# Seven block products in place of eight for the 512-row expert blocks of a Fourier-mixing and mixture-of-experts kernel

## The chip, the core and the metric

The kernel runs on one NeuronCore of one Trainium2 chip. The metric is the device time of one execution in microseconds (us). A NeuronCore has a matmul engine (PE, TensorE), three engines for elementwise work (DVE or VectorE, ACT or ScalarE, POOL or GpSimd), an engine that here only issues transfers (SP), and 16 DMA engines. Each engine takes its instructions in the order in which the program emits them, and waits on semaphores for the others. [...]

## What is computed

The input x has 8 batches of 2496 rows of 256 values. Each batch goes through a Fourier transform over its rows and then over its columns, of which the real part is kept. Each of the 19968 resulting rows then goes to one of 8 experts, two matrix products with a relu between them, and is multiplied by its gate probability:

```python
X = np.fft.fft(np.fft.fft(x, axis=1), axis=2).real     # 8 x 2496 x 256
x = X.reshape(19968, 256)
logits = x @ w_gate
expert_idx = np.argmax(logits, axis=1)
gate_w = softmax(logits)[rows, expert_idx]
for e in range(8):                                     # x_sorted: rows by expert
    h = np.maximum(x_sorted[lo:hi] @ w1[e], 0.0)       # 256 -> 1024
    y_sorted[lo:hi] = h @ w2[e]                        # 1024 -> 256
return gate_w[:, None] * y                             # rows in their first order
```

All of it is in fp32.

## The kernel before

**Front end.** `first(b)` loads a batch, folds its mirrored rows and columns on DVE (`fold` and `fold_d`, L242 to L258) and does the first stage of the row transform; its result goes out to DRAM (`Td`) and comes back regrouped. `second(b)` does the second stage and the column transform: matmuls into PSUM tiles of the pool `pm_` (three buffers), copies to `z` on ACT, and, per step, two slices of 128 finished rows, one copied on ACT (L339) and one on DVE (L340). `route` (L346) finds expert and gate of each of the 10 x 128 rows of half a batch by small DVE operations, ranks the rows by matmuls (`rk`), and scatters each slice of 128 rows into the DRAM table `Xs` by an indirect DMA that POOL issues (`put_row`, L176). A row of `Xs` has W = 258 values: 256 of the row, its number in the output, and its gate.

**Experts.** `Xs` holds the rows by expert. `plan` writes tables that say at which row of `Xs` each block starts and which expert it has. `rounds` fixes the order and the sizes of the blocks: 2 of 256 rows and 4 of 128 after the first batch, 4 of 256 after the second, then 3, 5, 5, 5, 5 and 5 of 512 after the others, and 21 of 256 at the end; 59 in all, 28 of them of 512. The blocks of one round run while the front end of the batch after next is worked in between.

For each block `fetch` (L438) has SP load its rows (`xb`) and both weight matrices of its expert (`w1_sb`, `w2_sb`, 1 MB each, two buffers each), one block ahead. `turn` (L451) transposes the rows on TensorE into a PSUM tile and copies it to `xT` on DVE (L460). In `experts` (L463) layer 1 of a 512-row block is eight chunks of two products: the stationary operand is 128 x 128 of w1, the moving one 128 x 512 of `xT`, and the results `ph` leave PSUM through a relu to `hT`, by turns on DVE (L499) and ACT (L501). Layer 2 is four tiles of 128 rows, each eight products: stationary 128 x 128 of `hT`, moving 128 x 256 of w2. Its result `py` leaves through ACT (L513), which multiplies each row by its gate, and POOL scatters the tile to the output rows (`put_row` again). The next block's transposes stand between the tiles of layer 2. Two PSUM buffers each serve `ph` and `py`.

**Order.** The order on every engine is the order of emission, written by hand with generators. `experts` yields after each chunk of layer 1 (weight 1) and each tile of layer 2 (weight 2), 16 for a 512-row block. The main loop (L600 to L614) spreads the steps of the front end (`mixed`) over the expert work of a round: TICKS = 44 steps over the first 70% of the round's weight. Every fp32 matmul of the program stands in the profile as two MATMUL instructions on line L162, each with a weight load (PEld).

Of the kernel before, what the change touches and what calls it, by code (L numbers as in the profile page):

```python
# [11 lines left out]
F32 = mybir.dt.float32  # L12
BF16 = mybir.dt.bfloat16
I32 = mybir.dt.int32
ALU = mybir.AluOpType
ACTF = mybir.ActivationFunctionType
# [3 lines left out]
B, S, D = 8, 2496, 256  # L20
# [8 lines left out]
BIG, BLK = 512, 256  # L29
CAP = NT + BLK  # L30
ROWS = E * CAP + BLK
W = D + 2
NSL = 2 * HG
NY = D + 1
OUT = 1.0e6
# [6 lines left out]
def bc(ap, axis, n):  # L42
    shape = list(ap.shape)
    shape.insert(axis, n)
    return ap[tuple([slice(None)] * axis + [None])].to_broadcast(shape)
# [89 lines left out]
    return plan  # L135


TICKS = 44
MOST = max(k for now in rounds() for _, k, _ in now)


# [15 lines left out]
def kernel(ctx: ExitStack, tc, x, w_gate, w1, w2, out):  # L157
    nc = tc.nc
    vec, act, pool = nc.vector, nc.scalar, nc.gpsimd

    def mm(o, lhsT, rhs, start=True, stop=True):
        nc.tensor.matmul(o, lhsT=lhsT, rhs=rhs, start=start, stop=stop)  # L162

    Td = [nc.dram_tensor(f"Td{b}", (NR, 16 * D), F32, kind="Internal").ap() for b in range(B)]
    Xs = nc.dram_tensor("Xs", (ROWS, W), F32, kind="Internal").ap()
# [30 lines left out]
    bp = ctx.enter_context(tc.tile_pool(name="bp", bufs=2))  # L196
    pm_ = ctx.enter_context(tc.tile_pool(name="pm_", bufs=3, space=PSUM))
    pst = ctx.enter_context(tc.tile_pool(name="pst", bufs=1, space=PSUM))
    psh = ctx.enter_context(tc.tile_pool(name="psh", bufs=2, space=PSUM))
    psy = ctx.enter_context(tc.tile_pool(name="psy", bufs=2, space=PSUM))  # L200

    ix = cp.tile([NA, B * 4], I32, name="ix")
    at = (np.arange(B)[:, None] * (S // 4) + 7 - np.arange(4))[None]
# [142 lines left out]
    def route(b, h, rows, lg):  # L346

        nonlocal base

        def small(name, *dims, dt=F32):  # L350
            return sp.tile([128, *dims], dt, tag=name, name=name)

        mx, eq, v = small("mx", NSL), small("eq", NSL, E), small("v", NSL)
        vec.reduce_max(mx[:], lg[:], axis=AX_X)
        vec.tensor_tensor(eq[:], lg[:], bc(mx[:], 2, E), op=ALU.is_equal)
        vec.tensor_tensor(eq[:], eq[:], bc(con["rev"][:], 1, NSL), op=ALU.mult)
        vec.reduce_max(v[:], eq[:], axis=AX_X)
        vec.tensor_tensor(v[:], v[:], con["good"][:, h], op=ALU.mult)
        oh = small("oh", NSL + 1, E, dt=BF16)
        vec.memset(oh[:, NSL], 0.0)  # L360
        vec.tensor_tensor(oh[:, 0:NSL], bc(con["rev"][:], 1, NSL), bc(v[:], 2, E), op=ALU.is_equal)
        yield

        su = small("su", NSL)
        vec.tensor_tensor(lg[:], lg[:], bc(mx[:], 2, E), op=ALU.subtract)
        act.activation(lg[:], lg[:], ACTF.Exp)
        rk = pm_.tile([128, NSL + 1, E], F32, tag="m", name="rk")
        mm(rk[:], tri[:], oh[:], True, False)
        for s in range(NSL):
            mm(rk[:, s + 1:], ones[:], bc(oh[:, s], 1, NSL - s), False, s == NSL - 1)  # L370
        yield
        vec.reduce_sum(su[:], lg[:], axis=AX_X)
        vec.tensor_scalar(su[:], su[:], 1e-9, None, op0=ALU.add)
        vec.reciprocal(rows[:, :, D + 1], su[:])
        vec.tensor_scalar(rows[:, :, D], con["row"][:, h], float(b * S), None, op0=ALU.add)
        pos, pf, pi = small("pos", NSL, E), small("pf", NSL), small("pi", NSL, dt=I32)
        vec.tensor_tensor(pos[:], rk[:, 0:NSL], bc(base[:], 1, NSL), op=ALU.add)
        vec.tensor_tensor(pos[:], pos[:], oh[:, 0:NSL], op=ALU.mult)
        vec.reduce_sum(pf[:], pos[:], axis=AX_X)
        vec.tensor_tensor(pi[:], pf[:], con["far"][:, h], op=ALU.add)  # L380
        nxt = cp.tile([128, E], F32, tag="base", name="base", bufs=2)
        vec.tensor_tensor(nxt[:], rk[:, NSL], base[:], op=ALU.add)
        base = nxt
        for s in range(NSL):
            sent(put_row(Xs, pi[:, s:s + 1], rows[:, s], E * CAP - 1, "xs"), b)
            yield

# [50 lines left out]
    def fetch(b, size, tab, i):  # L438
        n = size // 128
        row = nc.sync.value_load(tab[:, 0, i:i + 1], min_val=0, max_val=ROWS - size)  # L440
        ev = nc.sync.value_load(tab[:, 1, i:i + 1], min_val=0, max_val=E - 1)
        xb = bp.tile([128, BIG // 128, W], F32, tag="xb", name="xb")
        taken(nc.sync.dma_start(out=xb[:, 0:n].rearrange("p t c -> p (t c)"),
                                in_=Xs[ds(row, size)].rearrange("(p t) c -> p (t c)", t=n)), b)
        w1_sb = bp.tile([128, 2, F], F32, tag="w1", name="w1_sb")
        nc.sync.dma_start(out=w1_sb[:], in_=w1[ds(ev, 1)].rearrange("o (c p) f -> p (o c) f", p=128))
        w2_sb = bp.tile([128, FC, D], F32, tag="w2", name="w2_sb")
        nc.sync.dma_start(out=w2_sb[:], in_=w2[ds(ev, 1)].rearrange("o (c p) d -> p (o c) d", p=128))
        return xb, w1_sb, w2_sb

    def turn(size, xb):  # L451

        xT = bp.tile([128, 2, BIG], F32, tag="xT", name="xT", bufs=1)
        n = min(size // 128, 2)
        for h in range(-(-size // 256)):
            pt = pst.tile([128, 2, n, 128], F32, tag="t", name="pt")
            for c in range(2):
                for t in range(n):
                    nc.tensor.transpose(pt[:, c, t], xb[:, 2 * h + t, c * 128:(c + 1) * 128], ident[:])  # L459
            vec.tensor_copy(xT[:, :, 256 * h:256 * h + 128 * n], pt[:].rearrange("p c t k -> p c (t k)"))  # L460
            yield xT

    def experts(todo):  # L463

        got, xT = None, None
        for k, (b, size, last, at) in enumerate(todo):
            n, m = size // 128, BIG // size
            if not k:  # L470
                while todo[0][:3] not in tabs:
                    yield 0
                got = fetch(b, size, tabs[b, size, last], at)
                for _ in range(9):
                    yield 0
                for xT in turn(size, got[0]):
                    pass
            xb, w1_sb, w2_sb = got
            got, turned = None, iter(())
            follow = todo[k + 1] if k + 1 < len(todo) else None  # L480

            def fetch_next():
                b, size, last, at = follow
                return fetch(b, size, tabs[b, size, last], at)

            if follow and follow[:3] in tabs:
                got = fetch_next()
            ro = bp.tile([128, BIG // 128], I32, tag="ro", name="ro", bufs=4)
            vec.tensor_copy(ro[:, 0:n], xb[:, 0:n, D])
            hT = bp.tile([128, FC, BIG], F32, tag="hT", name="hT", bufs=1)  # L490
            for f in range(FC // m):
                ph = psh.tile([128, m, size], F32, tag="h", name="ph")
                for j in range(m):
                    for c in range(2):
                        mm(ph[:, j], w1_sb[:, c, (m * f + j) * 128:(m * f + j + 1) * 128], xT[:, c, 0:size],
                           c == 0, c == 1)
                o = hT[:, m * f:m * (f + 1), 0:size]
                if f % 2:
                    vec.tensor_scalar(o, ph[:], 0.0, None, op0=ALU.max)  # L499
                else:  # L500
                    act.activation(o, ph[:], ACTF.Relu)  # L501
                yield 1
            if follow:
                while follow[:3] not in tabs:
                    yield 0
                got = got or fetch_next()
                turned = turn(follow[1], got[0])
            y = bp.tile([128, BIG // 128, D], F32, tag="y", name="y", bufs=3)
            for i in range(n):
                py = psy.tile([128, D], F32, tag="y", name="py")  # L510
                for f in range(FC):
                    mm(py[:], hT[:, f, i * 128:(i + 1) * 128], w2_sb[:, f], f == 0, f == FC - 1)
                act.activation(y[:, i], py[:], ACTF.Copy, scale=xb[:, i, D + 1:D + 2])  # L513
                put_row(out, ro[:, i:i + 1], y[:, i], NT - 1, "out")
                if i < n - 1 or n == 2:
                    xT = next(turned, xT)
                yield 2
            for xT in turned:
                pass

    def pads(b):
# [78 lines left out]
    for b in range(1, B):  # L600

        side, done, due = mixed(b), 0, 0.0
        if b == 1:
            side = woven(close(0), chain(early, side))
        total = 16 * sum(k * size for size, k, _ in rounds()[b - 1]) / BIG
        while done < total:
            w = next(work)
            done += w
            due += TICKS * w / (0.7 * total) if w else 1
            while due >= 1:  # L610
                next(side, None)
                due -= 1
        for _ in side:
            pass  # L614
# [27 lines left out]
```

## Time and profile before

| what | value |
|---|---|
| median of 10 runs | 1524.75 us (1519.35 to 1527.54) |
| the profiled execution | 1524.91 us |
| its span, first to last instruction | 1522.7 us |
| TensorE busy | 1435.8 us, 94% of the span |
| DVE, ACT, POOL busy | 390.8, 283.8, 379.9 us |
| layer 1 of all blocks (`ph`, L162) | 1888 instructions, 612.6 us |
| layer 2 of all blocks (`py`, L162) | 2720 instructions, 616.0 us |
| scatters to `Xs` and to the output (L177) | 160 and 170, 165.4 and 165.9 us |
| mean granted TensorE clock | 0.979 |
| DMA traffic | 234.19 MB, mean 154 GB/s |

The page of a profile gives for each engine its busy time, then the span in 40 slices with a digit for the busy tenths, then groups of equal instructions: line, engine, operation, output<-inputs, count, total busy time, mean duration in ns, and the idle time of the engine before them with what ended it. A timeline gives start, duration, engine, line and operation of each instruction or run of equal ones. Matmuls are pipelined, so the duration of one is longer than the distance between two starts. The time before the first 200 us and the very end aside, TensorE is nearly always busy; in the first 150 us it is busy for 99.8 us.

### The profile page before, as it was taken

How to read it: one execution, taken by the hardware profiler on the slowest of the kernel's cores; microseconds unless marked ns; L12 is line 12 of the kernel's file. 1: busy time of each engine (PE TensorE's matmuls, PEld its weight loads, DVE VectorE, ACT ScalarE, POOL GpSimd, SP SyncE). 2: the span in 40 equal slices, each digit the busy share in tenths (PEclk: the TensorE clock that was granted, in tenths of full speed). 3: DMA queues.
4: the chain of work that ended last, by engine and by line, in shares of the span. 5: the costliest groups of instructions: out<-in, count | busy, mean ns of one | idle time of the engine just before them, and what ended most of it. 6: DMA issues, size and time to landing. Idle time of an engine off the chain costs nothing.

```text
span 1522.7 us, 16870 instructions
## 1 busy us (share of the span) xinstructions
PE 1435.8 (94%) x6108; PEld 1068.9 (70%) x6108; DVE 390.8 (26%) x1139; ACT 283.8 (19%) x598; POOL 379.9 (25%) x382
## 2 busy tenths in 40 slices
PE   4759798998999999999999999999999999999998
PEld 2537687776676657776677677666766788888887
DVE  3462233342232223322232212123111111111111
ACT  1212122122122211221122112111111111111111
POOL 2344314322314311324122311331421111111111
PEclk9869999999999999999999999999999999999999
DMA  7648667736336442553434422532352255465451
GB/s 179 175 148 257 206 203 222 254 89 187 120 109 206 153 145 87 160 179 124 155 114 139 152 90 87 178 112 100 130 173 87 85 197 177 165 202 183 167 194 63
DMA packets 126131, 234.19 MB, mean 154 GB/s; under 512 B 12829, under 2 KB 85648, under 8 KB 126048
## 3 DMA queue, kind: packets, MB, share of 16 engines
q1 hardware_dynamic: 103491, 178.31, 36.4%
q0 software_dynamic: 20192, 53.43, 10.6%
q10 hardware_dynamic: 2365, 1.38, 0.4%
q8 instruction: 48, 0.79, 0.2%
q14 instruction: 35, 0.29, 0.1%
HBM read 179.15 MB, written 56.28 MB: 155 GB/s over the span
## 4 chain that ended last, share of the span: by engine, by line
PE 50%; issue 30%; POOL 6%; DVE 1%; POOLq 0%; ACT 0%
PE py L162 20%; PE ph L162 20%; PE p L162 5%; POOL out_dram L177 4%; PE s L162 2%; POOL Xs L177 1%; PE pt L459 1%; POOLq L177 0%; PE rk L162 0%; DVE xT L460 0%; ACT hT L501 0%; DVE hT L499 0%; PE pr L162 0%; POOLq L637 0%; DVE rows L340 0%
## 5 line engine op out<-in xcount | busy, mean ns | idle before, releaser
L162 PE MATMUL ph<-xT,w_sb 128*128 128x512 f32 (+2 forms) x1888 | 612.6, 478 | 15.8 <-issue 6.6
L162 PE MATMUL py<-w_sb,hT 128*128 128x256 f32 x2720 | 616.0, 381 | 8.2 <-DVE hT L499 6.6
L162 PEld LDWEIGHTS py<-w_sb,hT 128*128 128x128 f32 x2720 | 512.8, 191 | 84.7 <-issue 8.4
L162 PEld LDWEIGHTS ph<-xT,w_sb 128*128 128x128 f32 x1888 | 349.9, 192 | 230.1 <-issue 183.6
L177 POOL DMA_INDIRECT out_dram<-y,ro x170 | 165.9, 976 | 890.5 <-ACT y L513 822.0
L499 DVE TENSOR_SCALAR hT<-ph 128x512 f32<-128x512 f32 x170 | 117.6, 692 | 643.4 <-PE ph L162 355.5
L513 ACT ACTIVATE y<-py,xb 128x256 f32<-128x256 f32 x170 | 80.7, 475 | 620.7 <-PE py L162 592.9
L177 POOL DMA_INDIRECT Xs<-rows,pi x160 | 165.4, 1034 | 105.0 <-issue 55.0
L501 ACT ACTIVATE hT<-ph 128x512 f32<-128x512 f32 x170 | 101.6, 598 | 387.2 <-PE ph L162 362.1
L460 DVE COPY xT<-pt 128x512 f32<-128x512 f32 (+1 forms) x87 | 59.1, 680 | 252.5 <-PE pt L459 246.8
L162 PE MATMUL p<-rd,z 128*128 128x273 f32 x320 | 93.8, 419 | 8.5 <-ACT z L333 6.3
L162 PE MATMUL s<-xh,w 78*80 78x256 f32 (+2 forms) x262 | 76.8, 422 | 26.3 <-DVE xh L247 18.7
L340 DVE COPY rows<-p 128x256 f32<-128x256 f32 x80 | 34.0, 425 | 182.2 <-ACT rows L339 169.2
L162 PEld LDWEIGHTS s<-xh,w 78*80 78x80 f32 x262 | 43.2, 172 | 47.8 <-DVE xh L247 18.9
L162 PEld LDWEIGHTS p<-rd,z 128*128 128x128 f32 x320 | 59.0, 202 | 22.5 <-ACT z L333 8.4
L237 POOL DMA_INDIRECT xh<-in_x_dram,ix x31 | 31.9, 1028 | 136.7 <-PE s L162 121.6
L162 PEld LDWEIGHTS p<-m,t 128*128 128x128 f32 x320 | 49.0, 205 | 23.7 <-issue 13.2
L162 PE MATMUL p<-m,t 128*128 128x128 f32 x320 | 52.6, 294 | 5.7 <-ACT z L333 2.2
L459 PE MATMUL pt<-ident,xb 128*128 128x128 f32 x340 | 52.0, 275 | 2.7 <-DMA xb<-Xs 2.7
L459 PEld LDWEIGHTS pt<-ident,xb 128*128 128x128 f32 x340 | 43.1, 143 | 12.3 <-DMA xb<-Xs 3.5
L270 ACT COPY t<-s 80x512 f32<-80x512 f32 x64 | 37.0, 581 | 64.7 <-PE s L162 55.5
L339 ACT COPY rows<-p 128x256 f32<-128x256 f32 x80 | 29.9, 373 | 53.7 <-PE p L162 50.4
(89 smaller groups left out, 327.4 us busy)
## 6 DMA issues: line engine op xcount, KB each, us to landing
w_sb<-in_moe_w_dram SPq DMA_DIRECT2D x118, 1024.0 KB
xb<-Xs SPq DMA_DIRECT2D x28, 516.0 KB
Td<-t SPq DMA_DIRECT2D x32, 320.0 KB
t<-Td SPq DMA_DIRECT2D x16, 640.0 KB
xl<-in_x_dram SPq DMA_DIRECT2D x31, 312.0 KB
xb<-Xs SPq DMA_DIRECT2D x27, 258.0 KB
out_dram<-y,ro POOLq DMA_INDIRECT x170
Xs<-rows,pi POOLq DMA_INDIRECT x160
```

What stands on the lines that cost most here:

```text
L162: nc.tensor.matmul(o, lhsT=lhsT, rhs=rhs, start=start, stop=stop)
L177: return unordered(pool.indirect_dma_start(out=dst, out_offset=bass.IndirectOffsetOnAxis(ap=idx, axis=0), in_=rows, in_offset=None, bounds ...
L237: pool.indirect_dma_start(out=xh[:].rearrange("p j d -> p (j d)"), out_offset=None, in_=xrows, in_offset=bass.IndirectOffsetOnAxis(ap=ix[: ...
L270: act.copy(t1[:, 2 * half:2 * half + 2], ps[:])
L339: act.copy(rows[:, k, 0:D], p3[:, 0:D])
L340: vec.tensor_copy(rows[:, k + 1, 0:D], free(p3[:], D, [-1, D]))
L459: nc.tensor.transpose(pt[:, c, t], xb[:, 2 * h + t, c * 128:(c + 1) * 128], ident[:])
L460: vec.tensor_copy(xT[:, :, 256 * h:256 * h + 128 * n], pt[:].rearrange("p c t k -> p c (t k)"))
L499: vec.tensor_scalar(o, ph[:], 0.0, None, op0=ALU.max)
L501: act.activation(o, ph[:], ACTF.Relu)
L513: act.activation(y[:, i], py[:], ACTF.Copy, scale=xb[:, i, D + 1:D + 2])
```

## The change

The 512-row blocks take both layers in another way. A matrix product whose factors are each cut in 2 x 2 parts needs eight products of parts. With sums and differences of parts, seven products do (the form with 15 sums of Strassen and Winograd). For each layer the program forms four such sums of the left factor (`left`) and four of the right one (`right`), runs seven products, and adds them up to the four parts of the result (`seven`): three products accumulate in PSUM onto banks that already hold another one, and DVE adds the rest in five sums.

Layer 1's left factor is w1 (its sums are made on POOL, in `turn` for the next block), its right one is `xT`, cut in two times 256 rows (sums on DVE). Layer 2's left factor is the hidden layer (sums on DVE, with a relu in some of them), its right one w2, cut into 128 columns (sums on POOL, at the block's start). Layer 1 works in two halves (`g`) of two chunks; each half has a tile of 512 values in each of four PSUM banks, a, b, c and d, which replace the buffers of `ph` and `py`. The order of the hidden layer's last sums is set by `late`.

The gate is applied to the rows before they are scattered to `Xs` (ACT, in `route`), not to the results; the gate is positive, so it passes through the relu. `Xs` loses its column for the gate, W is 257. `route` yields five times more in each half batch. A 512-row block now yields a weight of 14, and TICKS is 52. The blocks of 256 and 128 rows keep their products, in the new PSUM banks, and their results leave by a plain copy. The transposed rows of 512-row blocks are copied to `xT` on ACT.

```diff
-W = D + 2
+W = D + 1
-TICKS = 44
+TICKS = 52
+HALVED = (512,)
...
-    psh = ctx.enter_context(tc.tile_pool(name="psh", bufs=2, space=PSUM))
-    psy = ctx.enter_context(tc.tile_pool(name="psy", bufs=2, space=PSUM))
+    pse = ctx.enter_context(tc.tile_pool(name="pse", bufs=1, space=PSUM))
...
-        vec.reciprocal(rows[:, :, D + 1], su[:])
+        vec.reciprocal(su[:], su[:])
+        yield
...
         for s in range(NSL):
+            act.activation(rows[:, s, 0:D], rows[:, s, 0:D], ACTF.Copy, scale=su[:, s:s + 1])
             sent(put_row(Xs, pi[:, s:s + 1], rows[:, s], E * CAP - 1, "xs"), b)
...
+    def left(eng, o, a11, a12, a21, a22):
+        eng.tensor_tensor(o[0], a21, a22, op=add)
+        eng.tensor_tensor(o[1], o[0], a11, op=sub)
+        eng.tensor_tensor(a21, a11, a21, op=sub)
+        eng.tensor_tensor(o[2], a12, o[1], op=sub)
+        return a11, a12, o[2], a22, o[0], o[1], a21
+
+    def right(eng, o, b11, b12, b21, b22, sign):
+        eng.tensor_tensor(o[0], b12, b11, op=sub)
+        eng.tensor_tensor(o[1], b22, o[0], op=sub)
+        third = (b22, b12) if sign > 0 else (b12, b22)
+        eng.tensor_tensor(b12, *third, op=sub)
+        eng.tensor_tensor(o[2], b21, o[1], op=sub)
+        return b11, b21, b22, o[2], o[0], o[1], b12
+
+    def seven(shape, product, out12, out21, out22, done, late=()):
+        n = int(np.prod(shape))
+        bank = {k: pse.tile([128, *shape], F32, tag=k, name=k) for k in "abcd"}
+        a, b, c, d = (bank[k] for k in "abcd")
...
+        product(0, a, True)
+        yield
+        product(5, b, True)
+        p1, u2, u4 = temp("p1"), temp("u2"), temp("u4")
+        act.copy(p1, a[:])
+        yield
+        product(4, c, True)
+        vec.tensor_tensor(u2, p1, b[:], op=add)
+        yield
+        product(6, d, True)
+        vec.tensor_tensor(u4, u2, c[:], op=add)
+        yield
+        product(1, a, False)
+        vec.tensor_tensor(out22, u4, d[:], op=add)
+        done(11, a)
+        done(22)
+        for f in late[:-1]:
+            f()
+        yield
+        product(2, c, False)
+        yield
+        product(3, d, False)
+        vec.tensor_tensor(out12, u2, c[:], op=add)
+        done(12)
+        for f in late[-1:]:
+            f()
+        vec.tensor_tensor(out21, u2, d[:], op=add)
+        done(21)
+        yield
...
     def turn(size, got):
...
+        if halved:
+            ws = bp.tile([128, 3, F // 2], F32, tag="ws", name="ws", bufs=1)
+            l = left(pool, [ws[:, k] for k in range(3)], *(w1_sb[:, c, k] for k in range(2) for c in range(2)))
+            yield
...
+            r = right(vec, [xs[:, k] for k in range(3)],
+                      *(xT[:, c, k * th:(k + 1) * th] for c in range(2) for k in range(2)), 1)
...
+    def two_layers(size, got, lr, xb, ro):
...
+        r2 = right(pool, [wt[:, k] for k in range(3)],
+                   *(w2_sb[:, c, :, k * H:(k + 1) * H] for c in range(2) for k in range(2)), -1)
...
+            def sums12(h11=h11, h12=h12, h22=h22, s1=s1, s2=s2):
+                vec.scalar_tensor_tensor(s1, h12, 0.0, h22, op0=ALU.max, op1=add)
+                vec.tensor_tensor(s2, s1, h11, op=sub)
+
+            def sums34(h11=h11, h12=h12, h21=h21, s2=s2, s4=s4):
+                vec.scalar_tensor_tensor(h12, h12, 0.0, h11, op0=ALU.max, op1=sub)
+                vec.tensor_tensor(s4, h21, s2, op=sub)
+
+            if (g + 1) * fp == FC // 2:
+                late = late + [sums12]
+                yield from seven((fp, th), product, h12, h21, h22, done, late)
+                sums34()
+            else:
+                yield from seven((fp, th), product, h12, h21, h22, done)
+                sums12()
+                late = [sums34]
+        l2 = [hid[:, 0], hid[:, 2], hs[:, 2], hid[:, 3], hs[:, 0], hs[:, 1], hid[:, 1]]
...
+        yield from seven((nt, H), product, y[:, 0:nt, H:], y[:, nt:2 * nt, 0:H], y[:, nt:2 * nt, H:], done)
...
-        total = 16 * sum(k * size for size, k, _ in rounds()[b - 1]) / BIG
+        total = sum(k * (14 if size in HALVED else 16) * size / BIG for size, k, _ in rounds()[b - 1])
```

Layer 2's products use the banks of layer 1's parts in the same order; `l2` says which part or sum of the hidden layer each of the seven products has as its stationary operand (h11, h21, s4, h22, s1, s2, h12).

## The prediction

> **What bounds the kernel now.** I read the page's head and its 40 slices first, to see whether one engine fills the time; then tables by stretch, to see where it does not; then the groups kept apart by shape, and last the timeline, for the true spacing of instructions.
>
> ```profile
> span 1522.7 us, 16870 instructions
> PE 1435.8 (94%) x6108; PEld 1068.9 (70%) x6108; DVE 390.8 (26%) x1139; ACT 283.8 (19%) x598; POOL 379.9 (25%) x382
> PE   4759798998999999999999999999999999999998
> ```
>
> ```profile
> 200.00:300.00 100.00, 92.79 (x465) 77.76 (x464) 37.38 (x121) 22.42 (x51) 33.31 (x33) 0.97 0.66 215
> 723.32:751.74 28.42, 28.42 (x105) 19.02 (x105) 4.22 (x7) 4.29 (x8) 3.90 (x4) 1.00 0.33 112
> 1200.00:1300.00 100.00, 100.00 (x473) 86.94 (x472) 14.36 (x27) 14.89 (x28) 14.34 (x15) 1.00 0.47 157
> ```
>
> Columns of the second fence: stretch and its length, then busy time and count of PE, PEld, DVE, ACT and POOL, the granted clock, DMA. The middle line is one 512-row block with no front-end work beside it: PE is busy for all of its 28.42 us and DVE for 4.22. TensorE's columns are the bound; every other engine has room, until it is given work that TensorE must wait for.
>
> ```profile
> 658.07 3.60 PE L162 MATMUL ph<-xT,w_sb 128*128 128x512 f32 x8
> 661.51 0.61 PE L162 MATMUL p<-m,t 128*128 128x128 f32 x4
> ...
> 182.19 3.84 PE L162 MATMUL ph<-xT,w_sb 128*128 128x128 f32 x32 [0.52 <-DVE ro L489]
> 185.86 3.62 PE L162 MATMUL py<-w_sb,hT 128*128 128x256 f32 x16
> 189.32 0.38 PE L459 MATMUL pt<-ident,xb 128*128 128x128 f32 x2
> ```
>
> Starts count here, since durations overlap. An fp32 product is two instructions. 512 columns: 3.44/8 = 0.430 us each. 256 columns: 3.46/16 = 0.2163. 128 columns, new weights each: 3.67/32 = 0.1147. A transpose: 0.44/4 = 0.11. A block before is 32 x 0.430 + 64 x 0.2163 + 8 x 0.11 = 13.76 + 13.84 + 0.88 = 28.48 us, and the stretch above says 28.42.
>
> **TensorE's part.** Layer 1 becomes 7 products x 4 chunks x 2 instructions = 56 of 256 columns: 12.11 us. Layer 2 becomes 7 x 8 x 2 = 112 of 128 columns: 12.85 us. With transposes 25.84, so 2.64 less a block; 28 such blocks save 73.9 us. Layer 2 gains only 1.0 us of its 13.84, because 128-column instructions come at the pace of their weights. The bounds for one are 0.110 (transposes) and 0.118 (a stretch of 32 loads in 3.76 us at 163.5): 28 x 112 x 0.008 = 25 us between them. I take 0.1147, the nearest shape.
>
> **DVE's part.** It gets 18 sums of 512 elements in layer 1, 5 of 256 in layer 2 and 4 of 256 on xT, and loses four evictions of 512 and two copies.
>
> ```profile
> L499 DVE TENSOR_SCALAR hT<-ph 128x512 f32<-128x512 f32 x170 | 117.6, 692 | 643.4 <-PE ph L162 355.5 <-issue 257.0 <-remote 30.9
> L245 DVE TENSOR_TENSOR xh<-xl 78x508 f32<-78x508 f32 x31 | 21.1, 679 | 0.0
> L340 DVE COPY rows<-p 128x256 f32<-128x256 f32 x80 | 34.0, 425 | 182.2 <-ACT rows L339 169.2 <-issue 9.4 <-DMA Xs<-rows,pi 3.5
> ```
>
> A sum over 512 with one operand in PSUM is not in the trace; at 80 elements it costs the same as from SBUF (L377 235 ns, L378 242), so I take 0.70 with its gap, and 0.43 for 256. That is 12.6 + 2.15 + 1.7 + 0.16 = 16.6 us a block against 4.3. It fits inside 25.84, but not evenly: 12.6 of it falls on layer 1's 12.11 us of TensorE. I walked one lone block by hand in each engine's order, 0.2 us from a product's last column to its reader. Without further waits, u2, u4 and out22 stay ahead of the accumulation that needs their bank by 0.6 us or more; s2 of the second half ends at 13.96, just where TensorE wants it for layer 2's second product (12.12 + 1.84). Cost 0.1 us. With front-end work beside it, layer 1 gets some 3 us on TensorE (five blocks took 166.2 us between row fetches at 489.61 and 655.81; less 5 x 28.48 that is 24 a batch, over 3.7 blocks, half in each layer) and 3.45 on DVE (390.8 less 117.6 for hT, 59.1 for xT and 10 for ro, over 8 batches, is 25.5 a batch, spread likewise): 16.05 against 15.1, of which layer 2's first product covers some. I take 1.2 us a block; bounds 0 and 3. What is late then is s2, then product 5 of layer 2, and behind it in TensorE's queue the front end's matmuls.
>
> **POOL's part**, the disputed one. It gets eight sums of 512 a block: four on w2 at the block's start, behind the last block's four scatters, and four on the next w1, which wait for layer 1's last reader of ws. The trace has no elementwise POOL work. [...] What matters is what the two engines do to each other:
>
> ```profile
> 88.15 0.97 POOL L177 DMA_INDIRECT Xs<-rows,pi  x1 [9.06 <-ACT z L333]
> 89.43 1.92 POOL L177 DMA_INDIRECT Xs<-rows,pi  x1 [0.30 <-issue]
> ```
>
> ```profile
> 89.30 1.20 DVE L253 TENSOR_TENSOR xl<-xl,xh 78x1020 f32<-78x1020 f32 x1
> 90.43 0.15 DVE L412 SCALAR_TENSOR_TENSOR p_rb<-p_ex,bt 1x8 f32<-1x8 f32 x1
> ```
>
> A scatter that takes 0.97 alone takes 1.92 when it starts under a DVE sum of two SBUF tensors: it ends 0.85 after that sum does. So the sum shuts POOL out. The reverse shows in a DVE scalar operation (L373: median 174 ns, longest 438, beside a scatter at 683). Twelve of the new DVE operations read two SBUF tensors: s1, s2, h12, s4 of both halves, and the four on xT. I take it that POOL's sums shut these out, and walk the lone block again. w2's sums run from 4.2 to 9.3, and hold s1 and s2 of the first half (due at 6.96), so u4 comes at 12.0, 1.7 us after TensorE could use its bank. w1's sums start as layer 1 ends, just when s1 and s2 of the second half are due; the engines take turns, and product 5 starts 1.6 us late. Stall at 1.2 us a sum: 3.3; at 0.68: about 1.5 (only the second wait is left). I take 2.7, since at 99.5 DVE kept its turn for two sums together. It cannot be below 0 by this cause.
>
> [...]
>
> **The rest.** Copies, relus and xT copies on ACT: 2 x 4 x 0.6 + 1.2 + 0.75 = 6.75 us a block, hidden under TensorE; u2 waits for b later than for p1. Uncovered, p1's copies would cost 1.2. The gate on 160 row slices is 160 x 0.475 (L513's form) = 76 us of an ACT that is 19% busy; each hides under POOL's 1.28 us a send, uncovered it costs half a microsecond per group of ten. Route's five new yields and 52 ticks move the front end's end from 45 steps in 44 ticks, 72%, to 55 in 52, 74% of a round (steps counted in the code), with a block and more before the next round's first fetch. Before 150 us TensorE idles 50 us and order decides, so 5 us either way; I take 0. The 31 blocks of other sizes keep their instructions; SP's queue and the fetches are unchanged.
>
> **Sum.** Rounds of 3+5+5+5+5 blocks run beside a batch's front end, 74% of them: 17 blocks. The other 11 run alone. 11 x 2.7 + 17 x (2.7 + 1.2) = 29.7 + 66.3 = 96.0 of stalls, less 73.9: +22.1. The profiled span becomes 1544.8; that execution took 1524.91, 2.2 more than its span, and the median is 1524.75, so no further correction: 1547 us.
>
> **Rivals.**
> First, POOL's sums do not hold DVE. For it: no row shows them doing so. Against: both rows above show the two engines excluding each other. Stalls 11 x 0.1 + 17 x 1.2 = 21.5, so -52: 1472 us. Chance 0.33.
> Second, one wait only per pair, or POOL's sum at DVE's pace. For it: 99.5. Stalls 11 x 1.5 + 17 x 2.7 = 62.4, so -11: 1513 us; below the old time by little. Chance 0.15.
> Third, on the slow side and by another road: POOL as the bound. If a sum costs over 2.3 us, eight plus nine DMA issues at 1.28 pass 30 us a block and w2's sums come after layer 2 wants them; at 2.6 it is 32.3 us where 25.84 + 3 was needed: 28 x 3.5 - 74 + 21 = +45: 1570 us. [...] Chance 0.07.
> That seven products are not issued is no rival: 56 and 112 instructions a block stand in the changed program's order.
>
> **From these to numbers.** Forecast 0.45, within 1525 to 1590. The second rival reaches both sides. A change under 0.2%, 3 us, can't be told from none. Faster: 0.33 + 0.08 = 0.41; same 0.04; slower 0.55. The range takes the first rival in: 1468 to 1590; the likeliest's own is 1525 to 1590.
>
> **What would show it.** TensorE's spacing in layer 2: 0.1147. [...] DVE's s1 and s2 longer than 0.70 or starting late, beside POOL sums. TensorE waiting for DVE's u4 and s2, some 2.7 us a lone block. A lone block of 28.5 us (25.9 if the first rival holds); five-block rounds of some 170 us against 166.2. The forecast falls if s1 and s2 keep 0.70 beside POOL's sums.

## The result and the profile after

The changed kernel takes 1610.69 us (median of 9 runs, 1604.53 to 1616.85) against 1524.34 us for the kernel before in the same session: a ratio of 1.0566, 95% interval 1.055 to 1.0582. It is slower, as forecast, but by 86 us and not by 22: 1611 lies above the whole range. The profiled execution took 1613.85 us. First the head of its page, with the slices of TensorE and of its granted clock:

```profile
span 1611.8 us, 22447 instructions
PE 1404.9 (87%) x8124; PEld 1238.0 (77%) x8124; DVE 815.6 (51%) x1727; ACT 397.4 (25%) x870; POOL 696.8 (43%) x606
PE   4757798787899888999899889988988999999998
...
PEclk9868998999899999999999999999989999999999
```

TensorE has 31 us less to do than before and a share that is 7 points lower: there are holes now where the rounds run. Then the table by stretch over the 512-row blocks, from the first one's first matmul to the last one's last, for the kernel before and the one after (columns as in the prediction; the third from the end is the granted clock):

```profile
297.73:1217.00 919.27, 907.25 (x3592) 621.03 (x3593) 236.84 (x676) 177.47 (x376) 238.56 (x241) 1.00 0.41 133
```

```profile
314.20:1306.00 991.80, 876.21 (x5609) 786.49 (x5608) 662.98 (x1264) 272.72 (x587) 552.15 (x460) 0.96 0.37 123
```

The stretch starts 16.5 us later and is 72.5 us longer; what follows it is the same. In it TensorE stands still for 115.6 us (991.80 less 876.21), not for 12.0, and its clock is 0.96. Where it waits, from the view of waits (sum, times, longest; some records are missing):

```profile
PE c L163 <- DVE u L499: 39.2, 23, 5.7
PE b L163 <- DVE hs L581: 24.8, 13, 4.2
...
PE d L163 <- DVE hid L502: 8.7, 4, 2.8
```

These are u4 and s2, the two the forecast named. The groups show the pair behind them, the sums of DVE that read two SBUF tensors (those of the pools without `space=PSUM`) and POOL's sums of weights (count, busy, mean ns):

```profile
L581 DVE TENSOR_TENSOR hs<-hs,hid 128x512 f32<-128x512 f32 x56 | 66.3, 1184 | 1.9
L463 POOL TENSOR_TENSOR ws<-ws,w_sb 128x512 f32<-128x512 f32 x28 | 42.8, 1528 | 2.2
...
L502 DVE TENSOR_TENSOR hid<-u,d 128x512 f32<-128x512 f32 x56 | 38.4, 686 | 7.5 <-PE a L163 1.4 <-PE d L163 0.9 <-issue 0.9
```

s2 (L581) takes 1184 ns; a sum of the same size with one operand in PSUM, where the matmuls of both kernels put their results, takes 686 (L502). In one lone block the two engines hold each other up by turns (timeline: start, duration):

```profile
1229.41 1.27 POOL L471 TENSOR_TENSOR wt<-w_sb,wt 128x512 f32<-128x512 f32 x1
1230.43 0.80 DVE L580 SCALAR_TENSOR_TENSOR hs<-hid 128x512 f32<-128x512 f32 x1
1230.64 1.71 POOL L473 TENSOR_TENSOR w_sb<-w_sb 128x512 f32<-128x512 f32 x1
1231.27 1.64 DVE L581 TENSOR_TENSOR hs<-hs,hid 128x512 f32<-128x512 f32 x1
1232.32 1.72 POOL L474 TENSOR_TENSOR wt<-w_sb,wt 128x512 f32<-128x512 f32 x1
```

POOL's L473 starts under s1 (L580) and ends at 1232.35, 1.12 after it; s2 (L581), started meanwhile, ends 0.56 after that; L474, started under s2, ends 1.13 after s2. Each ends 0.13 to 0.18 us less than its undisturbed time (1.27 for L473 and 1.31 for L474 in e4, 0.69 for s2 in e6) after the end of the other.

**Two kinds of chips.** The later runs fell on several chips. On three the kernel before takes 1484 to 1487 us, on three others 1522 to 1534 as above, so ratios are compared, and only between runs with a like time of before. None of these chips was met in two sessions, so chip and session can't be told apart; "kind of chip" stands for both. The kernel after was run again:

> The changed kernel once more, beside the others of this group. If all of its loss is the kernel's own, the ratio to the time before is 1.0566 again (1.05-1.06). If the part before the first 512-row block (+16.5 us) and the waits without a releaser are that chip's, the ratio is 1.03-1.045 where the time before is near 1486, and a lone block is 28.4 us all the same.

It fell on a chip of the first kind, with 1487.05 us before, and took 1537.05 us, 1.0338 (1.0317 to 1.0358). So some 50 us are the kernel's own and some 36 come from the kind of chip; the experiments take them one after the other.

### The profile page after: what moved, and what is told of

It is laid out like the page before. It is cut to its first block, busy times and chain, and to the rows that moved or that the text cites. A ratio compares the mean times of both kernels' runs of the same rounds, so it can differ in the third digit from the quotient of the medians.

```text
span 1611.8 us, 22447 instructions
## 1 busy us (share of the span) xinstructions
PE 1404.9 (87%) x8124; PEld 1238.0 (77%) x8124; DVE 815.6 (51%) x1727; ACT 397.4 (25%) x870; POOL 696.8 (43%) x606
## 5 line engine op out<-in xcount | busy, mean ns | idle before, releaser
L163 PE MATMUL ph<-xT,w_sb 128*128 128x256 f32 (+1 forms) x992 | 217.3, 377 | 16.2 <-DVE p_nb L411 5.4
L163 PEld LDWEIGHTS ph<-xT,w_sb 128*128 128x128 f32 x992 | 185.2, 198 | 42.3 <-ACT hid L675 5.8
L163 PE MATMUL py<-w_sb,hid 128*128 128x256 f32 x928 | 209.9, 379 | 2.9 <-DVE hid L673 2.9
L163 PEld LDWEIGHTS py<-w_sb,hid 128*128 128x128 f32 x928 | 174.1, 190 | 26.0 <-DVE hid L673 3.3
L163 PE MATMUL a<-xT,w_sb 128*128 128x256 f32 x448 | 119.0, 389 | 7.5 <-issue 3.5
L163 PE MATMUL a<-w_sb,hid 128*128 128x128 f32 x896 | 112.6, 277 | 4.9 <-issue 4.8
L163 PEld LDWEIGHTS a<-w_sb,hid 128*128 128x128 f32 x896 | 108.2, 193 | 8.4 <-issue 6.8
L163 PEld LDWEIGHTS a<-xT,w_sb 128*128 128x128 f32 x448 | 83.6, 194 | 22.1 <-ACT p L493 6.6
L163 PE MATMUL c<-xT,ws 128*128 128x256 f32 x224 | 62.8, 405 | 24.7 <-DVE u L499 18.2
L163 PE MATMUL c<-w_sb,hs 128*128 128x128 f32 x448 | 63.9, 303 | 21.0 <-DVE u L499 21.0
L163 PE MATMUL b<-wt,hs 128*128 128x128 f32 x448 | 58.5, 279 | 24.8 <-DVE hs L581 24.8
```

## The experiments

All times in this section are medians of three rounds beside the kernel before, except where a single profile is named. Times expected in us were written for a chip like that of the first result; where a run fell on the other kind, the ratio counts.

### One partner away

First, the weight sums left out (e1); second, DVE's two-SBUF sums left out (e4):

```diff
-            l = left(pool, [ws[:, k] for k in range(3)], *(...))
+            l = a11, a12, a12, a22, a22, a11, a21
...
-        r2 = right(pool, [wt[:, k] for k in range(3)], *(...), -1)
+        r2 = b11, b21, b22, b21, b11, b22, b12
```

> The changed kernel without POOL's sums of w1 and w2 (the seven products take the plain parts in their place, so the result is another one); everything else as it is. Exclusion (POOL's sums and DVE's sums of two SBUF tensors shut each other out): a lone block falls from 28.4 to about 25.6 us, s2 (L581) from 1.18 to 0.70, and the whole from 1611 to 1500-1530. DVE overload (its own 16.6 us a block are too much): the lone block stays above 28, the whole above 1590. Late answers (ACT and DVE act late while POOL issues DMAs in a row): only POOL's runs get shorter; the long waits without a releaser in the trace stay, the whole at 1540-1580.

```diff
-            r = right(vec, [xs[:, k] for k in range(3)], *(...), 1)
+            r = b11, b21, b22, b21, b11, b22, b12
...
-                vec.scalar_tensor_tensor(s1, h12, 0.0, h22, op0=ALU.max, op1=add)
-                vec.tensor_tensor(s2, s1, h11, op=sub)
+                pass
```

> The changed kernel without DVE's sums of two SBUF tensors (s1, s2, h12, s4 and the four on xT; the products take plain parts, so the result is another one), with POOL's sums in place. Exclusion: no partner is left except the front end's folds, so a lone block is 25.6 us, POOL's sums take 1.27-1.30 each, and the whole is 1500-1530, as without POOL's sums. DVE overload: DVE has 7.2 us a block less and the whole falls to 1500 too, but the kernel without POOL's sums does not. Late answers: 1540-1580.

Measured, before 1486.29 us: e1 1416.20 us, 0.9528 (0.9512 to 0.9544); e4 1441.37 us, 0.969 (0.9671 to 0.971). A lone block takes 25.47 us in e1 and in e4, and POOL's sums take 1.27 to 1.35 us in e4. Taking away either engine's half of the pair turns 3.4% slower into 3 to 5% faster. e1 gained more than expected: 121 us against the 1537 of its kind of chip, where 80 to 110 were forecast. The stretch of the 512-row blocks again, in the kernel before, the kernel after and e1, all on chips of the first kind:

```profile
270.05:1176.20 906.15, 903.00 (x3591) 621.42 (x3592) 236.82 (x676) 177.15 (x375) 237.98 (x241) 1.00 0.41 135
```

```profile
270.88:1230.39 959.51, 866.40 (x5608) 785.16 (x5607) 666.70 (x1264) 273.11 (x587) 556.81 (x462) 0.96 0.39 130
```

```profile
270.95:1108.24 837.29, 826.68 (x5608) 761.98 (x5607) 539.01 (x1264) 270.70 (x587) 234.84 (x238) 1.00 0.45 148
```

The three lines split the change. Fewer columns: 903.00 to 826.68, 76.3 us saved. Standing still: 959.51 less 866.40 is 93.1, against 3.2 before, 90.0 us lost. And the same 5608 matmuls take 866.40 us of busy time when TensorE has to wait between them and 826.68 when it has not: 39.7 us lost, with a granted clock of 0.96. The sum, 90.0 + 39.7 - 76.3 = 53.4, is the stretch's growth. Of the third term some 29 us are the clock: 60.6 us of the busy time lie where the granted clock is 0.50, 3.4 in e1, and a matmul there takes 0.223 us in place of 0.1115 (below), so half of it is counted as lost, an estimate. Some 7 more are an estimate too: TensorE stops 77 times and not 33, and at each stop the last matmul shows its whole duration (0.275 us in e1) and not its spacing (0.112). The other 4 are open. The third term shows in single places; this is the kernel after on that chip:

```profile
537.80 1.26 POOL L463 TENSOR_TENSOR ws<-ws,w_sb 128x512 f32<-128x512 f32 x1
537.98 0.34 DVE L431 TENSOR_REDUCE p_rw<-p_val 1x21 f32<-1x189 f32 x1
...
539.03 1.27 POOL L464 TENSOR_TENSOR w_sb<-w_sb 128x512 f32<-128x512 f32 x1
539.10 1.22 DVE L437 TENSOR_SCALAR p_n<-p_ex 1x8 f32<-1x8 f32 x1
540.26 1.26 POOL L465 TENSOR_TENSOR ws<-w_sb,ws 128x512 f32<-128x512 f32 x1
540.36 1.18 DVE L438 SCALAR_TENSOR_TENSOR p_n<-p_n,p_nb 1x8 f32<-1x8 f32 x1
...
541.65 0.40 DVE L499 TENSOR_TENSOR u<-u,c 128x256 f32<-128x256 f32 x1
...
542.11 3.78 PE L163 MATMUL c<-w_sb,hs 128*128 128x128 f32 x16 [4.67 <-DVE u L499]
...
545.68 2.32 PE L163 MATMUL d<-wt,hid 128*128 128x128 f32 x16
```

The same two products undisturbed, in the same run, and the clock granted behind the wait (columns as in the tables by stretch):

```profile
402.08 1.95 PE L163 MATMUL c<-w_sb,hs 128*128 128x128 f32 x16
403.87 1.95 PE L163 MATMUL d<-wt,hid 128*128 128x128 f32 x16
```

```profile
539.62:546.45 6.83, 4.34 (x20) 4.34 (x21) 3.21 (x6) 0.00 (x0) 1.90 (x2) 0.50 0.60 199
```

After a wait of 4.67 us, 16 matmuls take 3.57 us from start to start, 0.223 each; undisturbed ones take 0.1115. The same lines show what made u4 (L499) late there: the plan's operations of 8 elements, 0.15 us when free, take 1.2 us each beside POOL's sums, and they stand ahead of u4 in DVE's queue. The slow matmuls go with the granted clock: 0.223 against 0.1115 at 0.50. The length of a wait does not tell by itself whether the clock falls: of the 14 stretches at half clock among the 512-row blocks of this run, two follow a wait of 1.81 us with none longer in the 8 us before them, while other waits of 1.81 us are followed by none.

### Both partners away

The two edits above together.

> Leaves out both partners: the products take plain parts of w1, w2, xT and the hidden blocks, so POOL has no sums and DVE has no operation with two SBUF operands in a 512-row block (its sums with one PSUM operand stay). If the cost comes only where the two meet, taking away the second partner gains next to nothing after the first: a ratio of 0.945 to 0.955 (beside 0.953 without POOL's sums alone), five-block rounds of about 150 us, a lone block of 25.5. If each engine's added work costs by itself (rival), the two gains add: 1.034 less 0.081 less 0.065 is 0.89.

Measured, before 1525.01 us: 1498.91 us, 0.9848 (0.9819 to 0.9878). The figure of 0.95 was written for the other kind of chip. Beside the kernel after on its own kind, 1.0566, it gains 7.2%, where e1 gained 8.1% on the other; the two gains of 8.1 and 6.5% do not add. DVE's sums cost next to nothing alone. POOL's alone leave e4 25 us above e1, of the 121 that the two cost together; what they meet there was not traced. It is the meeting that costs most.

### The gate and the pace

The gate left out (e2); the old TICKS and none of `route`'s new yields (e3):

```diff
-            act.activation(rows[:, s, 0:D], rows[:, s, 0:D], ACTF.Copy, scale=su[:, s:s + 1])
```

> The changed kernel without the ACT instruction that multiplies each row slice by its gate (the results lack the gate). The step as predicted (hidden under POOL's sends): within 5 us of 1611. Rival: the gate makes ACT late for the front end, and the first 512-row block, 16.5 us later than before, comes back to about 300: 1595 or less.

```diff
-TICKS = 52
+TICKS = 44
...
-        yield
```

> The changed kernel with the old spreading of the front end: 44 ticks and without the five new yields in route. As predicted (order before 150 us is worth 5 us either way): 1606-1616. Rival: the new yields move the first batches' route behind other work and cost most of the 16.5 us before the first 512-row block: 1595 or less, with that block at about 300. Or the yields keep DVE's bursts apart, and without them the rounds get longer: above 1620.

Measured, before 1486.29 us: e2 1527.35 us, 1.027 (1.0253 to 1.0287); e3 1540.44 us, 1.0358 (1.034 to 1.0376). The kernel after has 1.0338 (1.0317 to 1.0358). The pace makes no difference beyond the intervals. The gate costs some 0.7%, 10 us; 4 of them lie ahead of the first 512-row block, which starts at 266.8 us and not at 270.9.

### The sums in another place, or on another engine

e7 keeps POOL's eight sums and puts them behind s4 of the block, when DVE's sums of the hidden layer are done (second buffers for `wt`, a small copy on POOL that waits for s4). e6 gives all eight to DVE, for the next block, during layer 2.

```diff
+            if tail:
+                pool.tensor_copy(ws[:, 0, 0:1], tail[0])
             l = left(pool, ...)
+            wt, r2 = w2_sums(got, pool)
```

> The changed kernel with all eight of POOL's sums for the next block after this block's last hidden sum (POOL waits for s4), so in layer 2, where DVE has only four short sums of two SBUF tensors (two buffers for wt and for y). Exclusion: s1, s2, h12, s4 take 0.70, a lone block is 26-27 us, the ratio 0.98-1.01. If what hurts is POOL's load and not the place of its sums: a lone block of 28 us or more, and a ratio of 1.03 or more.

```diff
-            l = left(pool, ...)
+            l = left(vec, ...)
...
+            _, r2 = w2_sums(got, vec)
```

> The changed kernel with POOL's sums moved to DVE: w1's and w2's for the next block, all during layer 2 of this one (two buffers for wt, two for y in place of three, for space). DVE then has 22 us of sums a block. Exclusion: with no partner on POOL each sum takes 0.70, layer 2 has room for eight more, a lone block is 25.5-26.5 us and the ratio to the time before 0.96-0.985. DVE overload: beside the front end DVE has 29 of some 32 us, TensorE waits for it, and the ratio is 1.00 or more.

Measured, before 1487.05 us: e7 1505.62 us, 1.0128 (1.0111 to 1.0145); e6 1437.63 us, 0.9673 (0.9656 to 0.9689), which beats both kernels. In e6 DVE does 12 sums of two SBUF tensors and 8 of weights in a block, and none is held: s2 (here L590) takes 693 ns and a lone block 25.47 us, as without any weight sums. So DVE's load was not the trouble.

```profile
L590 DVE TENSOR_TENSOR hs<-hs,hid 128x512 f32<-128x512 f32 x56 | 38.8, 693 | 1.9
```

e7 frees s2 (710 ns) and only moves the meeting. Its groups:

```profile
L163 PE MATMUL c<-w_sb,hs 128*128 128x128 f32 x448 | 67.2, 312 | 54.7 <-DVE u L499 54.7
L474 DVE TENSOR_TENSOR xs<-xT,xs 128x256 f32<-128x256 f32 x28 | 40.9, 1460 | 0.0
L473 DVE TENSOR_TENSOR xT<-xT 128x256 f32<-128x256 f32 x28 | 40.7, 1453 | 0.0
```

The xT sums, 419 ns in e6, take 1453 to 1460 beside POOL's sums, and TensorE waits 54.7 us for the u4 of layer 2 behind them. To see if that is all, e9 takes e7 and leaves the xT sums out (the edit on `r` of e4):

> POOL's sums stand behind s4 as in the run that moved them (ratio 1.013), and the four sums on xT are left out (the products take plain parts of xT). In that run TensorE waits 54.7 us for u4 of layer 2, and the xT sums stand in DVE's queue before u4 at 1.4 to 1.5 us each beside POOL's sums. If these are what holds u4, those 54.7 us fall below 10 and the ratio to 0.96 to 0.975. If POOL's sums hold the front end's small DVE operations for as long (rival), half or more of the wait stays and the ratio is 0.99 or above.

Measured, before 1525.01 us: 1556.07 us, 1.0205 (1.0178 to 1.0232). On that kind of chip no ratio of e7 exists, so the figures expected are not comparable; the wait is. It falls from 54.7 to 16.4 us, not below 10. What is left there looks like this (e9):

```profile
578.83 1.25 DVE L425 TENSOR_TENSOR p_eq<-p_ei,bt 1x189 f32<-1x189 f32 x1
580.04 1.36 DVE L427 SCALAR_TENSOR_TENSOR p_val<-bt,p_rb 1x168 f32<-1x168 f32 x1
...
586.85 3.36 PE L163 MATMUL c<-w_sb,hs 128*128 128x128 f32 x14 [3.83 <-DVE u L499]
```

So most of e7's wait was the xT sums, and the rest the plan's operations, the rival's cause. In every place tried for POOL's sums (the kernel after, e7, e9) some DVE operation met them.

### The other kind of chip

> The same kernel as the run with all weight sums on DVE, beside these on their chip: 0.966 to 0.969 if the gain does not hang on the chip. If it does (rival), a ratio off by 0.005 or more.

Measured, before 1525.01 us: 1535.11 us, 1.0077 (1.0053 to 1.0102); on the other kind the same kernel was at 0.9673. The gain does hang on the chip. Since both traces hold the same instructions in the same order, the n-th matmul of one can be put beside the n-th of the other. They run to the microsecond alike, but for some twelve places where the second falls behind, 95 us in all, net of what it makes up in between. The same for the kernel after is 76.0 us, for the kernel before 40.4. The difference of the last two, 35.6, is what the first result has beyond 1.0338. Of the 40.4 of the kernel before some 28 lie ahead of the first 512-row block (297.73 against 270.05) and some 13 in the stretch of the 512-row blocks, though a lone block takes 28.4 us on both; its second run (1484.36 us, once) was expected to show all of it ahead of the blocks and in the front end's waits. One such place, in e6 first on the faster chip and then on the slower one:

```profile
499.15 0.56 ACT L493 COPY p<-a 128x512 f32<-128x512 f32 x1
499.20 1.16 POOL L178 DMA_INDIRECT Xs<-rows,pi  x1 [0.30 <-issue]
...
499.75 0.69 DVE L496 TENSOR_TENSOR u<-p,b 128x512 f32<-128x512 f32 x1 [0.24 <-ACT p L493]
...
501.81 0.60 ACT L582 ACTIVATE hid<-a 128x512 f32<-128x512 f32 x1 [1.29 <-PE a L163]
```

```profile
553.57 0.56 ACT L493 COPY p<-a 128x512 f32<-128x512 f32 x1
553.62 1.15 POOL L178 DMA_INDIRECT Xs<-rows,pi  x1 [0.30 <-issue]
...
555.95 0.69 DVE L496 TENSOR_TENSOR u<-p,b 128x512 f32<-128x512 f32 x1 [2.03 <-PE d L163]
...
558.72 0.69 DVE L499 TENSOR_TENSOR u<-u,c 128x512 f32<-128x512 f32 x1 [2.08 <-remote]
...
564.37 0.60 ACT L582 ACTIVATE hid<-a 128x512 f32<-128x512 f32 x1 [9.43 <-PE d L163]
```

u2 (L496) follows p1's copy after 0.04 us in the first, after 1.82 in the second, and ACT's next relu (L582) starts 10.8 us after that copy, not 2.7. In both POOL issues 13 or 14 indirect DMAs in a row there, and every one of the larger gaps lies at such a row. The 330 scatters are the same in all kernels; the kernel before loses 1 to 5 us at such a row after 300 us. It has a second PSUM buffer to go on with, which may be why; no run gave the changed kernel one.

The gate once more, now without POOL's sums (e6 without L391):

> All eight weight sums on DVE, as in the run at 0.967, without the 160 ACT operations that multiply the sent rows by their gate: the rows are sent unweighted. If the gate delays the sends and with them the next row fetches, whatever the sums do, the ratio falls by 0.004 to 0.01, to about 0.96, and the 512-row stretch starts some 3 us earlier. If the gate is hidden and only DVE and POOL meeting made it seem to cost (rival), it stays at 0.966 to 0.968.

Measured, before 1525.01 us: 1531.76 us, 1.005 (1.0027 to 1.0072) against 1.0077 (1.0053 to 1.0102) for e6 with the gate. The intervals overlap: undecided, and at most some 0.6%.

Then the sends were spread: one more step of the round after each of a slice's sends (e11 is e6, e12 the kernel after, e13 the kernel before with a copy on ACT in the gate's place), over 85% of a round.

```diff
-TICKS = 52
+TICKS = 72
...
             sent(put_row(Xs, pi[:, s:s + 1], rows[:, s], E * CAP - 1, "xs"), b)
             yield
+            if b:
+                yield 1
...
-            due += TICKS * w / (0.7 * total) if w else 1
+            due += TICKS * w / (0.85 * total) if w else 1
```

> All weight sums on DVE, and every send of a row slice is followed by one more step of the round (72 steps in 85% of a round, not 52 in 70%), so that POOL's row sends no longer come in rows of ten and more. On a chip whose before takes about 1525 us the same kernel without this took 1.0077, and its matmuls follow those of the chip with 1487 us to the microsecond but for some twelve places, 7 to 13 us each, where POOL issues 8 to 24 indirect DMAs in a row. If such a row is what makes the other engines answer late, those in the 512-row part (some 60 us) shrink to a third or less and the ratio falls to 0.98 or below. If the chip is late for another reason (rival), it stays at 1.00 to 1.01. On a chip with about 1487 us both expect 0.963 to 0.972.

> The changed kernel with the same spread of its sends, POOL's weight sums in place. On a chip whose before takes about 1525 us: 1.0566 without it, of which some 45 us lie in rows of sends in the 512-row part; if the rows cause them, 1.025 to 1.04; rival: 1.05 to 1.06. On a chip with about 1487 us: 1.03 to 1.037 by both, and a change of that size either way would mean that the spread works by another road, such as fewer sends between POOL's sums.

> The kernel before with its sends spread in the same way (64 steps in 85% of a round, and a copy on ACT, in place and times one, ahead of each send, so that POOL cannot run ahead). On a chip with about 1525 us: rows of sends cost it some 12 us after 300 us (its matmuls have a second accumulator to go on with), so at best 0.992 to 0.998; the 25 us before 300 us stay, since the first batch's sends are not spread. Rival: 0.998 to 1.006. On a chip with about 1487 us: 0.998 to 1.006.

Measured, before 1534.0 us: e11 1531.34 us, 0.9986 (0.9968 to 1.0004); e12 1580.44 us, 1.0302 (1.0263 to 1.034); e13 1540.38 us, 1.0044 (1.0027 to 1.006). e12 came down from 1.0566 as expected, e11 by 0.9% only, e13 went up, as the rival had it. In e11 the longest rows in the rounds of five have 7 or 8 sends and no longer 13, and no gap of TensorE lies beside them; but a new wait has come, for the next block's rows, since the plan now ends late (e11's waits):

```profile
PE pt L544 <- DMA xb<-Xs: 29.7, 7, 11.6
```

In e6 on the slower chip that wait was 4.9 us. e14 and e15 are e11 and e12 with 70% again, and with the last batch's pad rows one per four steps:

```diff
-            due += TICKS * w / (0.85 * total) if w else 1
+            due += TICKS * w / (0.7 * total) if w else 1
...
-    for _ in work:
-        next(rest, None)
+    for k, _ in enumerate(work):
+        if k % 4 == 0:
+            next(rest, None)
```

> As the run with DVE sums and spread sends, with the front end back in 70% of a round (72 steps), and the last batch's pad rows sent one per four steps. In that run the rows of sends in the rounds shrank from 13 to 7 and left no wait of TensorE above 0.9 us beside them, but the round's plan then ended late: TensorE waits 11.6 and four times some 2.9 us for a block's rows (24 us) and four times some 2.5 us for a u4 that stands behind the plan's small DVE operations. If these are what was lost, on a chip with a before of 1525 to 1534 us the ratio falls from 0.9986 to 0.98 to 0.99. If late answers still hold it (rival), it stays at 0.995 to 1.005. On a chip with about 1487 us: 0.962 to 0.97.

> The changed kernel, POOL's weight sums in place, with its sends and pads in the same way (72 steps in 70% of a round, pads one per four steps). With 85% it took 1.0302 on a chip with 1534 us, of which some 24 us lay in late row fetches: 1.01 to 1.025 if these go and nothing else comes. If POOL's sums and the sends only change places in POOL's queue (rival), 1.03 to 1.04. On a chip with about 1487 us: 1.015 to 1.035.

Both fell on a chip of the first kind, before 1486.96 us: e14 1433.55 us, 0.9647 (0.9626 to 0.9668), the lowest ratio of the kernels that leave nothing out, though its interval overlaps that of e6; e15 1504.53 us, 1.0115 (1.0095 to 1.0135), better than either theory had it. TensorE's idle time in e15's stretch is 75.9 us against 93.1; which of the changed places gave that was not tried. e14 was run once more:

> The kernel at 0.9647 on a chip with a before of 1487 us, once more, for a chip with about 1525 to 1534 us, which it did not get. If the rows of sends and the late row fetches were what held its fellow at 0.9986 there: 0.98 to 0.99. If late answers hold it whatever the rows (rival): 0.995 to 1.005. On a chip with about 1487 us it repeats 0.963 to 0.967 and settles nothing.

Measured, before 1522.6 us: 1503.87 us, 0.9882 (0.9842 to 0.9923), where e6 had 1.0077. The wait for rows is back at 4.7 us. So e14's kernel takes less time than both kernels on both kinds of chip, 3.5% and 1.2% less than the kernel before. Set beside its own run on the other kind, matmul by matmul, it still falls behind by 67 us, again beside rows of sends.

That the lateness lies at these rows is shown. That shorter rows mean less of it is not. In the last run the rows in the rounds of five are not short: 11 or 12 sends, or 7 and 6 with a pause between them, at two places in a round (11 to 15 in e14 on the other kind). Yet at such a place it loses 0.8 to 3.4 us, where e6 lost 6 to 7 and made up 2 or 3 of them later. e12's gain of 2.6% need not be less lateness, since e15, with a like spread, gained 2.2% on the kind of chip that is not late. e13 gained nothing. So what made the last kernel better on the late kind is open, and so is why that kind is late. Its traces hold none of the landings of POOL's 378 indirect DMAs, the others 190 to 378 of them, so the recording itself may have a part in it; that was not tried.

## Why the forecast was right in sign and wrong in size

**TensorE's part: right.** 73.9 us were to be saved; 76.3 were. Layer 2's spacing is 1.78 us for 16, 0.1115 and not 0.1147, within its bounds. A lone block without stalls takes 25.47 us (e1) where 25.84 was worked out.

**POOL's part: the mechanism right, the size of a sum wrong, the stall near by luck in part.** The two engines' sums hold each other up in both directions: s2 takes 1184 ns beside POOL's sums and 693 without them (e6), a POOL sum 1.5 us when held (L463, 1528 ns) and 1.27 to 1.35 undisturbed (e4). No run shows the 1.2 us a POOL sum with which the term of 2.7 was walked, nor the 0.68 under it; they were the author's figures, and the kernel before has no such sum. Nor does a run show 2.7 of waits on a lone block: they are 2.2 us. A lone block was to take 28.5 us and takes 28.4. Five-block rounds were to grow by 4 us and grew by 7 to 8 on the first kind of chip (164.7 to 171.8 and 172.9); the round of three, which has a whole front end beside it, by 21.8 (113.0 to 134.8). The stalls were to be 96.0 us in all; TensorE's idle time grew by 90.0. That 96 and 90 agree is in part luck: of the lone block's two waits the one at product 5 was to be 1.6 us and is 1.8, but the one for u4 was to be 1.7 and is 0.25, and the long waits at the ends of rounds came from operations that the sum did not count.

**DVE's part: incomplete.** The 1.2 us a block beside the front end counted its operations at their free durations. The plan's small operations and the xT sums are held as well, up to 1.2 us for one of 0.15, and they stand ahead of u4 at the turn of each round. The stall of 2.7 was put on every block alike, where it is 2.2 us of waits on a lone one and 5 at one go at a round's end.

**The sum: this is the step that failed.** It subtracted columns from stalls and left TensorE's pace as it was. With stalls of 2 to 5 us between them the same matmuls take 39.7 us more, some 29 of it at a halved clock. On a chip of the first kind 22.1 were forecast and 53.4 measured in the stretch: 39.7 for the pace, less 6.0 for smaller stalls, less 2.4 for more columns saved, is 31.3, all of the difference.

**"I take 0" for the rest: partly wrong.** Pace and yields: nothing beyond the intervals, right. Gate: some 10 us beside POOL's sums, not hidden. Start-up: 270.9 against 270.1 us on the first kind of chip, right; 16.5 us on the other, outside the 5.

**The chip.** The remaining 36 us were in no step. The profile before had them in part: its matmuls, too, fall 40.4 us behind those of a faster chip at rows of scatters. One profile alone could not tell that from the kernel's own time; what it could show is that `ph` and `py` had two buffers each and a, b, c and d have one.

**The rivals.** The first (POOL's sums do not hold DVE, 1472 us) fell with s2 at 1184 ns, though e6, 49.4 us under the kernel before on the first kind of chip, shows that its outcome, 52, was to be had by giving POOL no sums. The second (one wait per pair) nearly holds on a lone block (1.8 us at s2, 0.25 at u4); it fell on the rounds, where both waits are there and long, u4's the longer in all (39.2 against 24.8 us). The third (POOL as the bound) fell with a sum of 1.5 us, not 2.3, and with POOL at 43%.

## What to carry to other kernels

Before work goes to an idle engine, ask which running instructions of another engine it will hold up or be held up by (here s2 at 1184 ns in place of 693), small ones in the same queue included; here the sums were cheaper on a busy DVE (673.5 us of the stretch in e6, against 539.0 without them) than on an idle POOL. Price a wait of TensorE at more than its length, since the matmuls behind it can be slower (here 39.7 us on top of 90.0 of waiting). A kernel with one PSUM buffer where the old one had two may be more open to lateness (here 6 to 7 us at a long row of sends in e6, 1 to 5 in the kernel before; not tried apart from the rest), so time it on more than one chip.

## What the runs showed of the hardware that was not expected

DVE operations of 8 elements are held too: a TENSOR_SCALAR on 1 x 8 (L437) took 1.22 us in place of 0.15, and ended 0.02 us after the POOL sum beside it (L464). A reduction (L431) took its free 0.34 us beside such a sum (L463).

Chips, or sessions on them, differ. The same kernel before takes 1484 to 1534 us, and the same e6 is 3.3% faster than it on one chip and 0.8% slower on another; the difference lies in about a dozen places, beside rows of eight or more indirect DMAs that POOL issues. Rows of five or six show none of it in e6.

TensorE's granted clock was at half after waits as short as 1.81 us, and 90 us of waits in many pieces cost an estimated 29 us more by it.
